# Attention with hashed buckets and a product layer: one factor operation for all pairs of heads, more operations allowed on GpSimd, and a new order

## The chip, the cores and the metric

The kernel runs on one core of one Trainium2 chip. Its time is the device time of one execution in microseconds. Beside it stands the span of a profiled execution, from its first instruction to its last. Engines are named as in the profile: PE is TensorE (PEld its weight loads), DVE is VectorE, ACT is ScalarE, POOL is GpSimd, SP is SyncE, which issues the DMAs.

## What is computed

```python
q, k, v: (4, 8, 768, 64)    proj: (64, 6)
q_bucket = sum(2**i * ((q @ proj)[..., i] > 0))         # 6 bits, the same for k
scores = where(q_bucket[:, :, :, None] == k_bucket[:, :, None, :], q @ k.T / 8, -1e9)
attn = exp(scores - max(scores));  attn /= sum(attn) + 1e-9
x = (attn @ v), heads side by side: (3072, 512)
out = ((x @ w_a) * (x @ w_b)) @ w_out                   # w_a, w_b (512, 1536), w_out (1536, 512)
```

## The kernel before, in words

Everything is done in four batches of 8 heads. A batch's queries are taken in chunks of one or two tiles of 128 rows (14 chunks in all, `CHUNKS`); each chunk has one or two halves of 8 tiles of queries (`UT`), and for each tile the scores of 768 keys are made, exponentiated, transposed and multiplied with the values. When a chunk is done, its rows go through the product layer (`moe`), with the weights resident in SBUF.

Most products are made of two float16 parts each. `power_of` finds a power of two that bounds a tensor: a Gram matrix on PE (in batch 0; squares on ACT later), its largest element on DVE (`st_k`, `st_q`, `vst`), a sum over partitions on PE (`ps_k`, `ps_q`), and two small operations on DVE (`po_t`, then `ai`: the power and its inverse). The high half is the tensor times that power in float16 (`scaled`), on ACT or DVE; the low half is what remains, on DVE (a SCALAR_TENSOR_TENSOR). `split` does that for queries and keys (tiles `qt`, `kt`), turns both halves with the rows on partitions into columns (`turn(1)`, giving `trq`, `trk`), multiplies the columns by the projection (`kb`, `qb`), takes bits of the signs (`neg_k`, `neg_q` on ACT, `bits_k`, `bits_q` on DVE), writes them as a one-hot part beside a copy of the high half (`hp`), and turns that too (`turn(0)`). In the first batch keys of all four pairs of heads and the first queries are turned by PE (transposes, copied back by ACT or DVE), later ones by DMA. The scores (`s`) then hold the penalty for unequal buckets.

`qtile` makes one tile's scores: their largest value on DVE (`mx`), a scale (`sc`) and a bias (`bias`), and the exponential on ACT (`e`). The scale holds the factor `cq`, which undoes the powers of the queries and of the keys of that pair of heads: one DVE operation for each half of a chunk and pair (line 1147), 56 in all.

The weights come in pieces of 512 KB through three staging places; each pair of pieces is rewritten by three operations (`to_f32`: a low part on ACT or POOL, a high part on ACT, and their combination on DVE, all under the name `wz`), and the next pieces wait for that. Later they are split into halves by `halved`.

No engine's order is left to chance: the program collects its operations in a list (`Plan.op`), and issues them by two tables written into the file: `ORDER`, the sequence of all operations, and `ENGINE_OF`, the engine of each that may run on several. What an operation may run on stands in its first argument (`"ACT DVE"`), and `free(b, ...)` adds POOL in batch 0 alone.

Of the kernel before, what the change touches and what calls it, by code (L numbers as in the profile page):

```python
# [20 lines left out]
P = 128  # L21
# [317 lines left out]
class Buf:  # L339
# [11 lines left out]
    @property  # L351
    def t(self):
        if self.real is None:
            if self.ring is not None:
                self.real = self.ring.pop(0)
                return self.real
            self.real = self.pool.tile(self.shape, self.dtype, tag=self.tag, name=self.name, bufs=self.bufs)
        return self.real
# [1181 lines left out]
```

## Time and profile before

| | before |
|---|---|
| median of 3 runs (lowest, highest) | 892.28 us (892.0, 892.59) |
| profiled execution, its time | 892.21 us |
| its span | 890.4 us |
| busy: PE, PEld | 869.0 us (98%), 672.4 us (76%) |
| busy: DVE, ACT, POOL | 631.1 (71%), 565.9 (64%), 438.0 us (49%) |
| chain that ended last | PE 70%, DVE 3%, issue 1% of the span |
| HBM read, written | 37.82 MB, 6.29 MB |

The busy share is that of the whole span. A stage is read by the view of stretches, which sums each engine's busy time between two moments; by the timeline, which has each instruction's start, its length, and the idle time before it with what ended it; and by the groups of instructions of one kind, which have their number and length.

### The profile page before, as it was taken

Reading aid. Unit: us, or ns where it says so; the run is one execution under the profiler, and the core shown is the slowest. Engines: PE = TensorE matmul, PEld = TensorE weight load, DVE = VectorE, ACT = ScalarE, POOL = GpSimd, SP = SyncE. Lnnn points to the kernel's source line nnn. Section 1 sums busy time; section 2 is a strip of 40 time slices with the busy share of each in tenths; the row PEclk is TensorE's granted clock in tenths of the full one; section 3 lists DMA queues with packets and bytes.
Section 4 is the critical chain, followed back from the end, with each engine's and each line's share of the span. In section 5 each row is a group of like instructions: output and inputs, shape, how many; then the busy total and the mean of one; then the engine's idle time right before and its main releaser. Section 6 shows DMA issues by size and latency. Waiting matters only on the chain.

```text
span 890.4 us, 24299 instructions
## 1 busy us (share of the span) xinstructions
PE 869.0 (98%) x9761; PEld 672.4 (76%) x9761; DVE 631.1 (71%) x1461; ACT 565.9 (64%) x1116; POOL 438.0 (49%) x371
## 2 busy tenths in 40 slices
PE   5899999999999999999999999999999999999998
PEld 4798777878777777777777777777777777777775
DVE  7998999988876766767776775767778576643311
ACT  6887767766657777667666675667676466644222
POOL 2444456447426556554454565545556457544111
PEclk9999999999999999999999999999999999999999
DMA  9989996899979979998977787799987666745100
GB/s 328 302 268 260 173 167 148 155 191 191 196 144 191 162 162 168 172 224 154 185 137 155 149 170 158 131 195 173 200 170 138 125 149 125 144 90 103 30 24 24
DMA packets 430433, 145.31 MB, mean 163 GB/s; under 512 B 404080, under 2 KB 422640, under 8 KB 430320
## 3 DMA queue, kind: packets, MB, share of 16 engines
q1 hardware_dynamic: 430160, 143.76, 79.5%
q8 instruction: 76, 1.25, 0.6%
q14 instruction: 37, 0.30, 0.1%
q10 hardware_dynamic: 160, 0.00, 0.0%
HBM read 37.82 MB, written 6.29 MB: 50 GB/s over the span
## 4 chain that ended last, share of the span: by engine, by line
PE 70%; DVE 3%; issue 1%; ACT 0%; DVEq 0%; ACTq 0%
PE ab L1371 35%; PE o L1436 17%; PE s L1136 10%; PE av L1205 8%; DVE vh L569 0%; DVE g L1400 0%; PE qb L709 0%; DVE mx L1156 0%; PE kb L709 0%; DVE hp L736 0%; DVE hp L739 0%; DVE ai_q L549 0%; DVE osb L569 0%; DVE kt L670 0%; PE ps_cx L768 0%
## 5 line engine op out<-in xcount | busy, mean ns | idle before, releaser
L1371 PE MATMUL ab<-xT,wz 128*128 128x256 f16 (+1 forms) x3456 | 377.2, 264 | 1.0 <-DVE g L1400 0.8
L563 POOL TENSOR_TENSOR a<-e,a 128x768 f16<-128x768 f32 x170 | 286.2, 1687 | 186.7 <-ACT a L560 84.0
L1371 PEld LDWEIGHTS <-wz 128*128 128x128 f16 x3456 | 310.4, 98 | 49.5 <-issue 1.5
L1177 ACT ACTIVATE e<-s,bias,sc 128x768 f32<-128x768 f32 x192 | 189.7, 988 | 110.3 <-DVE bias L1168 93.0
L1156 DVE TENSOR_REDUCE mx<-s 128x1 f32<-128x768 f32 x192 | 182.6, 953 | 53.2 <-PE s L1136 49.1
L1436 PE MATMUL o<-wz,g 128*128 128x512 f16 (+1 forms) x840 | 215.8, 392 | 0.2 <-DVE g L1400 0.2
L1416 POOL TENSOR_TENSOR g<-g,g 128x256 f16<-128x256 f32 x132 | 94.8, 718 | 191.1 <-ACT g L1411 185.5
L1136 PE MATMUL s<-trk,trq 76*128 76x384 f16 (+1 forms) x768 | 155.0, 327 | 2.4 <-ACT e L1177 1.8
L1400 DVE SCALAR_TENSOR_TENSOR g<-ab,ab,a 128x256 f32<-128x256 f32 x132 | 63.4, 480 | 105.1 <-ACT a L1392 87.2
L1205 PEld LDWEIGHTS <-at 128*128 128x128 f16 x3312 | 117.5, 98 | 16.5 <-issue 2.7
L1436 PEld LDWEIGHTS <-g 128*128 128x128 f16 x792 | 73.9, 98 | 68.7
L1392 ACT ACTIVATE a<-ab,ab 128x256 f32<-128x256 f32 x132 | 62.1, 470 | 99.5 <-PE ab L1371 86.6
L1205 PE MATMUL av<-vh,at 128*128 128x64 f16 x2208 | 121.9, 193 | 0.0
L1136 PEld LDWEIGHTS <-trq 76*128 76x128 f16 (+1 forms) x768 | 70.6, 98 | 44.1 <-issue 6.8
L1411 ACT CAST g<-g 128x256 f16<-128x256 f32 x132 | 53.0, 402 | 59.0 <-DVE g L1400 48.5
L560 ACT CAST a<-e 128x768 f16<-128x768 f32 x102 | 84.5, 829 | 3.0 <-DMA at<-a 1.2
L1205 PE MATMUL av<-vl,at 128*128 128x64 f16 x1104 | 62.4, 193 | 0.0
L1363 PE MATMUL ab<-xT,wz 128*128 128x128 f32 x384 | 49.4, 279 | 0.0
L560 DVE CAST a<-e 128x768 f16<-128x768 f32 x68 | 39.4, 580 | 14.0 <-ACT e L1177 14.0
L1363 PEld LDWEIGHTS ab<-xT,wz 128*128 128x128 f32 x384 | 46.2, 192 | 3.4 <-issue 2.2
L1168 DVE TENSOR_SCALAR bias<-mx,sc 128x1 f32<-128x1 f32 x181 | 38.8, 214 | 6.4
L1164 DVE TENSOR_SCALAR sc<-mx,cq 128x1 f32<-128x1 f32 x181 | 38.3, 211 | 4.8
(171 smaller groups left out, 793.7 us busy)
## 6 DMA issues: line engine op xcount, KB each, us to landing
rq<-in_q_dram SPq DMA_DIRECT2D x24, 256.0 KB, 3.5
rk<-in_k_dram SPq DMA_DIRECT2D x16, 384.0 KB, 3.9
wz<-in_moe_w_a_dram SPq DMA_DIRECT2D x12, 512.0 KB, 5.9
wz<-in_moe_w_b_dram SPq DMA_DIRECT2D x12, 512.0 KB, 5.0
wz<-in_moe_w_out_dram SPq DMA_DIRECT2D x12, 512.0 KB, 5.6
out_dram<-osb SPq DMA_DIRECT2D x24, 256.0 KB, 2.4
vr<-in_v_dram SPq DMA_DIRECT2D x12, 384.0 KB, 4.4
at<-a SPq DMA_TRANSPOSE x184, 3.6
```

The costliest lines, as they stand in the source:

```text
L560: {"ACT": nc.scalar.copy, "DVE": nc.vector.tensor_copy, "POOL": nc.gpsimd.tensor_copy}[e](out=out, in_=x)
L563: (nc.gpsimd if e == "POOL" else nc.vector).tensor_tensor(out=out, in0=x, in1=y, op=ALU.subtract)
L1136: nc.tensor.matmul(ps.t[:, jj, :HALF], lhsT=trq.t[rows, i, (2 * j + h) * nt + t], rhs=tr.t[rows, i, k0 : k0 + NT // 2].rearrange("p n s -> ...
L1156: lambda: nc.vector.tensor_reduce(out=mx.t[:, col], in_=halves(ps.t), axis=AX.XY, op=ALU.max, negate=True),
L1177: lambda: nc.scalar.activation(flat2(e.t), halves(ps.t), AF.Exp, bias=bias.t[:, col], scale=sc.t[:, col], accum_out=sm.t[:, u : u + 1],),
L1205: nc.tensor.matmul(av.t[:, u, :], lhsT=at.t[:, a + kt, :], rhs=w.t[:, h, kt, :], start=i == 0, stop=i == 3 * NT - 1,)
L1363: nc.tensor.matmul(pl.t[:, m, to], lhsT=wt32(m, cc, f), rhs=xt.t[:, cc * nt // NC, cc * nt % NC : cc * nt % NC + nt, :], start=cc == 0, st ...
L1371: nc.tensor.matmul(pl.t[:, m, to], lhsT=wt(m, wi, cc, f), rhs=xt.t[:, cc * nt // NC, xi, cc * nt % NC : cc * nt % NC + nt, :], start=i == ...
L1392: lambda a=a, pl=pl, gr=gr, sc_of=sc_of: nc.scalar.activation(a.t, pl.t[:, 0, :CH], AF.Copy, scale=sc_of(gr)),
L1400: lambda a=a, g32=g32, pl=pl, gr=gr, sc_of=sc_of: nc.vector.scalar_tensor_tensor(out=g32.t, in0=pl.t[:, 1, :CH], scalar=sc_of(gr + 1), in1 ...
L1416: lambda g=g, g32=g32, g_of=g_of: nc.gpsimd.tensor_tensor(out=g_of(g[1]), in0=g32.t, in1=g_of(g[0]), op=ALU.subtract),
L1436: nc.tensor.matmul(po[u].t.rearrange("p a b -> p (a b)"), lhsT=x()[:, us], rhs=w, start=f == 0 and i == 0, stop=f == NF - 1 and i == len(t ...
```

## The change

The factors `cq` of all pairs of a half are made by one operation: the keys' powers of a batch get one tile (`k_ai`, one row of two numbers for each pair), and the operation reads the inverses of its pairs from it. In the first chunk alone there is still one operation for each pair. That makes 27 operations where there were 56. The pool `po_ai` shrinks from 14 buffers to 10. High halves (of queries, keys and values in batch 0, and of weights) and the cast of a chunk's output in batch 0 may also run on POOL. The constants of the power are listed as waiting for the projection. And both tables are new.

```diff
 ORDER = (
-    2, 1, 75, 11, 76, 4, 3, 77, 5, 78, 79, 80, 81, 0, 12, 13, 14, 15, 6, 282, 281, 9, 10, 84, 27, 16, 82, 17, 83, 18,
+    1, 2, 4, 3, 75, 76, 5, 77, 9, 78, 11, 79, 80, 6, 7, 12, 13, 14, 279, 0, 15, 16, 17, 278, 280, 281, 81, 10, 84, 18,
...
+class Part(tuple):
+    @property
+    def t(self):
+        return self[0].t[:, self[1]]
...
-    op("DVE", 0.4, pw_consts, -79, w=["pw"])
+    op("DVE", 0.4, pw_consts, -79, r=[("pj", 0), ("pj", 1)], w=["pw"])
...
-        ai = keep or buf("po_ai", [P, 2], F32, f"ai_{name}", 14)
+        ai = keep or buf("po_ai", [P, 2], F32, f"ai_{name}", 10)
...
             nc.scalar.activation(out, x, AF.Copy, scale=by)
         else:
-            nc.vector.tensor_scalar(out=out, in0=x, scalar1=by, scalar2=None, op0=ALU.mult)
+            (nc.gpsimd if e == "POOL" else nc.vector).tensor_scalar(
+                out=out, in0=x, scalar1=by, scalar2=None, op0=ALU.mult
+            )
...
-            "ACT DVE", {"ACT": 0.3 + 0.83e-3 * size, "DVE": 0.24 + 0.54e-3 * size},
+            *free(b, ACT=0.3 + 0.83e-3 * size, DVE=0.24 + 0.54e-3 * size, POOL=0.2 + 1.01e-3 * size),
             high, key, r=[*toks, ai] + ["csb"] * len(first), w=[(pt[0], "hi"), *first], sbuf=True,
...
-            "ACT DVE", {"ACT": 1.24, "DVE": 0.75}, lambda e: scaled(e, hi(), z(), al_of(ai)),
+            "ACT DVE POOL", {"ACT": 1.24, "DVE": 0.75, "POOL": 1.24}, lambda e: scaled(e, hi(), z(), al_of(ai)),
...
-                "ACT DVE", {"ACT": 0.95, "DVE": 0.65}, lambda e: scaled(e, flat(vh), x(), al_of(ai)),
+                *free(b, ACT=0.95, DVE=0.65, POOL=0.95), lambda e: scaled(e, flat(vh), x(), al_of(ai)),
...
+        if hp == 0:
+            kinv[b] = buf("k_ai", [P, NPAIR, 2], F32, f"k_ai{b}")
...
-        if h == 0 and t == 0:
+
+        js = slice(j, j + 1) if m == 0 else slice(0, UT // 2 // nt)
+        if h == 0 and t == 0 and js.start == j:
+            hps = slice(hp, hp + js.stop - js.start)
             op(
                 "DVE", 0.16,
                 lambda: nc.vector.tensor_scalar(
-                    out=cq.t[:, j : j + 1], in0=inv_of(qinv[m, half]), scalar1=inv_of(kinv[b, hp]), scalar2=0.125,
+                    out=cq.t[:, js], in0=kinv[b].t[:, hps, 1], scalar1=inv_of(qinv[m, half]), scalar2=0.125,
                     op0=ALU.mult, op1=ALU.mult,
...
-                "ACT DVE", {"ACT": 0.65, "DVE": 0.44}, lambda e: cast(e, t2.t[:, :w], flat()), key, r=[x],
+                *free(b, ACT=0.65, DVE=0.44, POOL=0.65), lambda e: cast(e, t2.t[:, :w], flat()), key, r=[x],
```

What the tables do is seen in the order of the instructions. The first place is ACT, from its fifth instruction on: `hp`, `trq` and `trk` are the copies of the first queries' and keys' halves and of their turned columns, `wz` the weights. Before:

```order
L560 COPY hp_76<-qt_0_0_111 128x8x64
L560 COPY trq_0_153<-qt_0_0_143 128x1024
L560 COPY trk_0_168<-kt_0_0_155 128x1536
L876 ACTIVATE wz<-wz 128x1024 x2
L560 COPY hp_77<-kt_0_0_140 128x12x64
L727 COPY neg_k_0_229<-kb_0_199 128x72
L727 COPY neg_q_0_231<-qb_0_217 128x48
L866 ACTIVATE wz<-wz 128x1024
```

and with the change:

```order
L875 ACTIVATE wz<-wz 128x1024
L885 ACTIVATE wz<-wz 128x1024
L567 COPY hp_77<-kt_0_0_138 128x12x64
L567 COPY trk_0_187<-kt_0_0_148 128x1536
L567 COPY trq_0_205<-qt_0_0_161 128x1024
L736 COPY neg_k_0_210<-kb_0_189 128x72
L885 ACTIVATE wz<-wz 128x1024
L736 COPY neg_q_0_229<-qb_0_214 128x48
L885 ACTIVATE wz<-wz 128x1024
```

The weights' low and high part (lines 875 and 885) come ahead of the first copies, and a third part (line 885) stands between `neg_k` and `neg_q`.

The second place is DVE, from the second keys' largest element (`st_k_1`) on, with the halves of `kt_0_1` and the one-hot parts of the first pair. Before:

```order
L583 TENSOR_REDUCE st_k_1_189<-gram_k_1_171 128x1
L546 TENSOR_SCALAR po_t_k_1_194<-ps_k_1_191 128x1
L549 SCALAR_TENSOR_TENSOR ai_k_1_195<-pw,po_t_k_1_194 128x2
L569 TENSOR_SCALAR kt_0_1_212<-rk_1_138,ai_k_1_195 128x12x64
L670 SCALAR_TENSOR_TENSOR kt_0_1_212<-rk_1_138,ai_k_1_195,kt_0_1_212 128x12x64
L884 SCALAR_TENSOR_TENSOR wz<-wz 128x1024
L583 TENSOR_REDUCE st_k_3_242<-gram_k_3_235 128x1
L730 TENSOR_TENSOR bits_k_0_261<-kb_0_199,neg_k_0_229 128x72
L736 TENSOR_SCALAR hp_77<-bits_k_0_261 128x12x6
L739 TENSOR_SCALAR hp_77<-bits_k_0_261 128x12x6
```

and with the change:

```order
L592 TENSOR_REDUCE st_k_1_207<-gram_k_1_180 128x1
L893 SCALAR_TENSOR_TENSOR wz<-wz 128x1024
L553 TENSOR_SCALAR po_t_k_1_226<-ps_k_1_223 128x1
L556 SCALAR_TENSOR_TENSOR k_ai_135<-pw,po_t_k_1_226 128x2
L739 TENSOR_TENSOR bits_q_0_231<-qb_0_214,neg_q_0_229 128x48
L576 TENSOR_SCALAR kt_0_1_233<-rk_1_170,k_ai_135 128x12x64
L679 SCALAR_TENSOR_TENSOR kt_0_1_233<-rk_1_170,k_ai_135,kt_0_1_233 128x12x64
L592 TENSOR_REDUCE st_k_3_246<-gram_k_3_238 128x1
L739 TENSOR_TENSOR bits_k_0_248<-kb_0_189,neg_k_0_210 128x72
```

A weights' combination (line 893) and the query bits (`bits_q`, which need `neg_q`) come ahead of the second keys' halves.

The third place is PE, around the products that give the bits of the first pair (`kb`, `qb`). Before, from the second keys' Gram matrix on:

```order
L596 MATMUL gram_k_1_171<-rk_1_138 128x128
...
L534 MATMUL ps_k_1_191<-st_k_1_189,onesr 128x1
...
L534 MATMUL ps_k_1_191<-onev,onesr 128x1
...
L709 MATMUL kb_0_199<-pjw_67,trk_0_168 128x12
...
L709 MATMUL qb_0_217<-pjw_68,trq_0_153 128x12
...
L596 MATMUL gram_k_3_235<-rk_3_233 128x128
```

and with the change (weight loads and repeated rows are left out in both):

```order
L605 MATMUL gram_k_1_180<-rk_1_170 128x128
...
L718 MATMUL kb_0_189<-pjw_67,trk_0_187 128x12
...
L718 MATMUL qb_0_214<-pjw_68,trq_0_205 128x12
...
L541 MATMUL ps_k_1_223<-st_k_1_207,onesr 128x1
...
L541 MATMUL ps_k_1_223<-onev,onesr 128x1
...
L605 MATMUL gram_k_3_238<-rk_3_236 128x128
```

The sum of the second keys' bound (`ps_k_1`) has moved behind `qb`.

## Rows read from the trace of the kernel before

**Rows 1.** The page's first part: busy time, share of the span and instructions by engine.
```profile
PE 869.0 (98%) x9761; PEld 672.4 (76%) x9761; DVE 631.1 (71%) x1461; ACT 565.9 (64%) x1116; POOL 438.0 (49%) x371
```

**Rows 2.** View by stretches: from:to, length, busy us (instructions) of PE, PEld, DVE, ACT, POOL, clock.
```profile
0.00:10.00 10.00, 2.98 (x27) 2.42 (x28) 4.87 (x19) 2.62 (x6) 2.70 (x7) 1.00 0.82 283
10.00:20.00 10.00, 8.42 (x101) 7.78 (x100) 9.26 (x27) 9.46 (x12) 2.44 (x2) 1.00 1.04 358
20.00:28.00 8.00, 6.60 (x48) 5.03 (x46) 7.48 (x18) 6.11 (x8) 3.16 (x3) 1.00 1.02 356
28.00:40.00 12.00, 9.78 (x132) 7.92 (x131) 11.79 (x29) 9.96 (x15) 5.84 (x7) 1.00 0.98 290
40.00:62.00 22.00, 21.70 (x211) 19.51 (x211) 21.61 (x46) 18.84 (x34) 7.41 (x9) 1.00 0.83 271
62.00:294.00 232.00, 228.34 (x2805) 181.42 (x2803) 199.73 (x444) 161.54 (x304) 120.67 (x102) 1.00 0.93 183
294.00:880.00 586.00, 584.68 (x6411) 444.47 (x6409) 374.60 (x881) 354.93 (x738) 294.44 (x243) 1.00 0.75 143
```

**Rows 3.** Timeline of PE: start us, length us, line, operation, count, [idle before, releaser].
```profile
13.00 0.36 PE L709 MATMUL qb<-pjw,trq 128*128 128x12 f16 x8
...
14.56 1.46 PE L688 MATMUL kt<-identh,kt 128*128 128x128 f16 x12 [0.50 <-DVE kt L670]
...
21.93 1.44 PE L688 MATMUL kt<-identh,hp 128*128 128x128 f16 x12 [0.38 <-ACT trq L560]
23.17 1.48 PE L1136 MATMUL s<-trk,trq 76*128 76x384 f16 x4
...
26.16 0.84 PE L596 MATMUL gram_v<-v 128*128 128x128 bf16 x6
...
28.24 0.83 PE L688 MATMUL kt<-identh,kt 128*128 128x128 f16 x12
```

**Rows 4.** Factors and powers (min/median/max ns); POOL groups (busy us, mean ns).
```profile
L1147 DVE TENSOR_SCALAR cq<-ai_q,ai_k x56: 198/205/216, 19.8 to 727.4; 128x1 f32<-128x1 f32 x56
...
L549 DVE SCALAR_TENSOR_TENSOR ai_q<-pw,po_t_q x24: 220/233/1685, 5.5 to 725.8; 128x2 int32<-128x2 f32 x24
...
L563 POOL TENSOR_TENSOR a<-e,a 128x768 f16<-128x768 f32 x170 | 286.2, 1687 | 186.7 <-ACT a L560 84.0 <-DVE a L560 59.4 <-issue 13.1
...
L560 POOL CAST a<-e 128x768 f16<-128x768 f32 x14 | 13.3, 952 | 4.5 <-ACT e L1177 2.7 <-issue 1.6
```

**Rows 5.** Timeline of ACT, the first 16 us.
```profile
9.78 1.01 ACT L560 COPY trq<-qt 128x1024 f16<-128x1024 f16 x1 [2.93 <-PE qt L688]
11.16 1.44 ACT L560 COPY trk<-kt 128x1536 f16<-128x1536 f16 x1 [0.37 <-PE kt L688]
12.50 2.18 ACT L876 ACTIVATE wz<-wz 128x1024 f32<-128x1024 f32 x2
14.58 0.81 ACT L560 COPY hp<-kt 128x768 f16<-128x768 f16 x1
...
15.41 0.18 ACT L727 COPY neg_q<-qb 128x48 f32<-128x48 f32 x1
15.50 1.12 ACT L866 ACTIVATE wz<-wz 128x1024 int32<-128x1024 uint8 x1
```

**Rows 6.** Timeline of POOL: the first weights' low part.
```profile
8.68 1.90 POOL L868 TENSOR_SCALAR wz<-wz 128x1024 int32<-128x1024 uint8 x1 [6.78 <-DMA wz<-in_moe_w_a_dram]
```

**Rows 7.** Timeline of DVE, the first 16 us.
```profile
9.71 0.87 DVE L549 SCALAR_TENSOR_TENSOR ai_pj<-pw,po_t_pj 128x2 int32<-128x2 f32 x1
...
12.38 0.16 DVE L546 TENSOR_SCALAR po_t_k<-ps_k 128x1 f32<-128x1 int32 x1 [0.28 <-PE ps_k L534]
...
12.83 0.62 DVE L569 TENSOR_SCALAR kt<-rk,ai_k 128x768 f16<-128x768 f32 x1
13.49 1.02 DVE L670 SCALAR_TENSOR_TENSOR kt<-rk,ai_k,kt 128x768 f16<-128x768 f32 x1
14.42 1.22 DVE L884 SCALAR_TENSOR_TENSOR wz<-wz 128x1024 int32<-128x1024 int32 x1
```

More of the change, by code (lines that the diff above doesn't have):

```diff
@@ L628, in attention_moe, with split @@
         )
-    def split(raw, x, n, side, b, key, toks, tag, by_pe=()):
+    def split(raw, x, n, side, b, key, toks, tag, by_pe=(), keep=None):
         which = "kq"[side]
@@ L655, in split @@
             gram(lambda: raw.t[:, :size], size, key, toks, lambda: stat.t, stat, tag, f"{which}{x}")
-        ai = power_of([lambda: stat.t], [stat], f"{which}{x}", key, tag, True)
+        ai = power_of([lambda: stat.t], [stat], f"{which}{x}", key, tag, True, keep)
         def high(e):
@@ L1050, in kprep @@
         raw = load_pair(k, b, hp, f"rk_{b}_{hp}", key - 1)
-        trk[b, hp], kinv[b, hp] = split(raw, f"{b}_{hp}", NK, 0, b, key, [raw], tag, () if b else K_PE.get(hp, ()))
+        if hp == 0:
+            kinv[b] = buf("k_ai", [P, NPAIR, 2], F32, f"k_ai{b}")
+        trk[b, hp], _ = split(
+            raw, f"{b}_{hp}", NK, 0, b, key, [raw], tag, () if b else K_PE.get(hp, ()), Part((kinv[b], hp))
+        )
     def heads(m, half):
@@ L1147, in qtile @@
                 lambda: nc.vector.tensor_scalar(
-                    out=cq.t[:, j : j + 1], in0=inv_of(qinv[m, half]), scalar1=inv_of(kinv[b, hp]), scalar2=0.125,
+                    out=cq.t[:, js], in0=kinv[b].t[:, hps, 1], scalar1=inv_of(qinv[m, half]), scalar2=0.125,
                     op0=ALU.mult, op1=ALU.mult,
                 ),
-                key - 1, r=[qinv[m, half], kinv[b, hp]], w=[(cq, j)],
+                key - 1, r=[qinv[m, half]] + [(kinv[b], x) for x in range(NPAIR)[hps]],
+                w=[(cq, x) for x in range(UT // 2)[js]],
             )
```

453 rows, old and new, of tables (ENGINE_OF, ORDER) are left out of this document.

## The prediction

> **What bounds the kernel now.** The first view is the busy time of the engines: TensorE (PE) is busy 869.0 us of a span of 890.4 us, 98% [rows 1]. Neither the matmuls' number nor their shapes change (9761 before and after), so the time can move only by what PE does not do in the other 21.4 us, and by how fast its clock runs. The view by stretches says where these lie [rows 2]: 7.0 us idle in the first 10 us, 1.6 up to 20, 1.4 up to 28 (10.0 in all by 28), 2.2 from 28 to 40, 0.3 from 40 to 62, 3.7 from 62 to 294, 1.3 in the 586 us from 294 to 880, and about 4 at the end, where the last outputs leave. The start is therefore the stage to read. There the timeline of PE [rows 3] shows two things. Twelve transposes of 128x128 take 1.46 us at 14.56 and 1.44 at 21.93, and 0.83 us at 28.24: up to 28 us PE ran at half speed (1.2 GHz), from then on at 2.4, though the column of the granted clock in [rows 2] stands at 1.00 throughout. And the first matmul of scores starts at 23.17 us, behind a chain that passes through all engines. VectorE (DVE) is busy 11.79 of 12 us from 28 to 40 and 21.61 of 22 up to 62 [rows 2]: in the start it is as full as PE.
>
> The profiled execution took 892.21 us, 1.8 more than its span, and lies 0.07 us under the median of the three runs shown (892.28); the sum is made against 892.21. What a measurement of this kernel can tell from no change is about 0.2%, 1.8 us.
>
> **The change, part by part.** *From 294 us on* the rows of PE, ScalarE (ACT), GpSimd (POOL) and SyncE stand in the same order before and after, and DVE only lacks operations of 0.2 us while it is busy 375 of 586 us [rows 2]. This stretch costs and gives nothing, and so does the end: a lead or a delay at 294 us is the result.
>
> *One operation for the factor of queries and keys.* 56 operations of 0.205 us on DVE [rows 4] become 27. That takes 29 x 0.2 = 5.9 us from DVE over the span; of these 11 are of batch 0 (20 become 9) and some 4 more lie before 294 us, 15 x 0.2 = 3.1 us. They lie beside PE's work; they count only where DVE is the one that is waited for.
>
> *GpSimd for high halves and casts.* The new list gives it ten such operations: three high halves of queries, one of keys, two of values, two of weights, two casts of outputs. The list moves other operations too: 7 pairs of one-column operations (scale and bias) leave DVE for GpSimd, and 5 remainders, larger ones, go from GpSimd to DVE; I set these two against each other and a little more, and count DVE as about 2 us lighter up to 294 us, between 0 and 5.9. The trace has no high half on GpSimd. The nearest rows are its cast of 128x768, 0.95 us, and its subtraction of the same size, 1.69 us [rows 4]; I take 0.95, since the new operation reads one tensor, as the cast does, and keep 1.69 as the upper end. For the halves of queries, two thirds that size, either is a bound from above.
>
> *The new order at the start.* This I follow by hand with durations of rows. ACT now takes the first weights' low and high part (1.12 and 2.18/2 = 1.09) before it has copied anything of queries and keys, and they land at 8.68, when GpSimd starts on them now [rows 5, 6]. So: 8.68 + 1.12 + 1.09 = 10.9; copy of the keys' high half 0.81, 11.7; copy of the first keys (trk) 1.44, 13.1, where it ended at 12.6; of the queries (trq) 1.01, 14.15, where it ended at 10.8. PE takes its instructions in order: the query bits (qb, 0.36) now start at 14.2 instead of 13.00, and the bound of the second keys (ps_k), which had been ahead of them, stands behind them and ends at 14.7. On DVE its power of two follows, at 14.8 where it ran at 12.38 (0.16 and 0.22, 15.2 with the steps between), and then, new, the query bits, which wait for ACT: neg_k, as long as neg_q, 0.18, another weights' high part 1.09, neg_q 0.18, so 15.6. Behind this wait DVE holds the second keys' two halves: 15.6 + 0.2 + 0.62 + 1.02 = 17.5, where the low half ended at 14.5 [rows 7]. PE's second transposes of keys start at 17.5 instead of 14.56 [rows 3]: 2.9 us late.
>
> From there: transposes 1.46, ACT's copy 1.44, key bits 0.36 x 12/8 = 0.54, neg_k 0.18: 21.1. DVE meanwhile does a weights' combination of 1.22 and eight small operations of about 0.2 each (the size of the factor's and of the power's, [rows 4]): 20.4 with the steps between; GpSimd's high half of the fourth keys 0.95, 21.3; DVE's low half 1.02, then a second combination of 1.22 and seven small ones: 25.0. PE transposes 1.44, a Gram matrix of four products (0.84 for six [rows 3], so 0.56), and the first scores start at 27.1 instead of 23.17, 3.9 us late. In between PE has done one Gram matrix of values (0.84) more. So PE has 3.9 - 0.84 = 3.1 us more idle time by 28 us, all of it at half speed. What is left undone is then done at full speed, so it costs 3.1 x 0.83/1.44 = 1.8 us. From 28 to 40 us I find the waits about equal (by the same steps: 0.6 for a copy of the third keys, 1.0 for exponentials, 0.3 for one-hot parts, against 2.2 now). **Start: +1.8 us.** Bounds: +0.6, if the two weights' parts on ACT land early enough to cost nothing beyond the 2 us of the second half of this chain; +3.1, without the discount for the clock.
>
> *GpSimd beside DVE.* The same DVE operation, the two numbers of a power of two, takes 0.22 us as a rule and 0.87 at 9.71 us, while GpSimd's operation of 8.68 to 10.58 runs [rows 6, 7]; the longest took 1.69 [rows 4], as long as a GpSimd subtraction. So each GpSimd operation in the start can hold a DVE operation with two inputs for 0.65 us; I count one such in the path at half its size: **+0.3 us**, between 0 and 1.3 (two at full size). The Trainium skill, SBUF — State Buffer, section Who interferes with whom, states that a VectorE instruction with two SBUF inputs and a GpSimd instruction that reads SBUF exclude each other for the whole instruction; by it the block in the path counts at its full 0.65, and the sum would be +2.5 rather than +2.1. No run here yet shows a high half beside it.
>
> *From 40 to 294 us* PE idles 4.0 us now. DVE is 2 us lighter, but is waited for in small pieces; I take 0, and bounds of -2.0 (half of the idle time gone) and +2.0 (a placement as much worse).
>
> The sum is 1.8 + 0.3 + 0 = +2.1: 892.2 + 2.1 = **894.3 us**; its own range is 893.2 to 895.6.
>
> **The rivals.** *Paid back.* The lighter DVE gives back in 40 to 294 us what the start loses, up to 2 of the 4.0 us: 892.2 us, 891 to 893.2. For it: DVE at 98% from 28 to 62 us [rows 2]. Against: PE idles only 0.3 us from 40 to 62, so there is little to be had just there.
>
> *Faster.* The chain above is too slow by some 2 us because an operation stands less in the way than I count, the start is then even, and DVE's lightness closes two thirds of the 4.0 us: 892.2 - 2.6 = 889.6. It decides if the first scores start before about 24 us. For it: the new order does its Gram matrices of values in gaps at half speed. Against: the waits on neg_q and on GpSimd's half are plain in the order.
>
> *The clock rises later.* PE had worked without a gap from 21.93 us when the clock rose at 28 [rows 3]. In the new order I find a gap up to 25.0, 3 us later. If the rise comes 3 us later too, PE's work in these costs (1 - 0.83/1.44) x 3 = 1.3 more: 895.6. The Trainium skill, TensorE: Matmul & The Clock Gate, Part 1, says that half speed is the resting state and that sustained work releases it, with a moment that varies from run to run. By that page this rival is open until a run shows it; the three runs, 0.6 us apart, speak against much chance in it.
>
> *More on GpSimd than it can hide.* With halves of 1.69 instead of 0.95 us, four of them before 62 us that DVE waits for, 4 x 0.74 = 3.0 more: 897.3.
>
> *The change does not do what it says.* It does, as far as an order can tell: 27 factors, and ten operations on GpSimd that it could not have before.
>
> **How the numbers follow.** Forecast 0.36 (of it 0.08 under 894.0, within 0.2%); paid back 0.24; faster 0.22; later clock 0.10; GpSimd 0.08. Slower by over 0.2%: 0.28 + 0.18 = 0.46; within: 0.08 + 0.24 = 0.32; faster: 0.22. The range runs from 889.2, which takes in the faster case's own time and leaves out what lies below it, to 897.5.
>
> **What would show it.** Right: the first scores start near 27 us, DVE waits for neg_q at 15 us, PE's idle time by 28 us is near 13 us, and from 294 us on every row lies later by the same 2 us. Wrong: the first scores before 24 us, transposes at 0.83 us well before or after 28, or PE idle time from 40 to 294 us far from 4.0.

## The result: 0.84% slower, in four pieces

The changed kernel takes 899.49 us (median of 4 runs, 899.34 to 900.1), the one before 892.14 us (4 runs, 891.62 to 892.59): the ratio is 1.0084, its 95% interval 1.0066 to 1.0101. The direction was forecast, the size (+2.1 us) was not, and 899.49 lies outside the range of 889.2 to 897.5. The profiled execution of the changed kernel took 899.34 us, its span is 897.5 us, 7.1 more than before.

The first part of its page, and the view by stretches with the same bounds as in [rows 2]:

```profile
PE 869.7 (97%) x9761; PEld 671.9 (75%) x9761; DVE 629.7 (70%) x1416; ACT 568.2 (63%) x1121; POOL 449.2 (50%) x382
```

```profile
0.00:10.00 10.00, 2.13 (x19) 1.66 (x20) 4.11 (x18) 2.77 (x5) 2.96 (x7) 1.00 0.82 276
10.00:20.00 10.00, 7.13 (x81) 6.50 (x79) 7.47 (x27) 8.11 (x11) 1.95 (x2) 1.00 1.04 400
20.00:28.00 8.00, 5.70 (x56) 4.54 (x54) 5.08 (x13) 5.58 (x7) 3.24 (x2) 1.00 1.04 324
28.00:40.00 12.00, 9.71 (x139) 8.51 (x138) 10.38 (x24) 11.36 (x16) 1.70 (x3) 1.00 0.54 176
40.00:62.00 22.00, 21.60 (x215) 19.43 (x213) 19.04 (x41) 19.89 (x36) 11.18 (x13) 1.00 0.98 296
62.00:294.00 232.00, 226.58 (x2762) 180.06 (x2762) 199.50 (x414) 157.76 (x296) 128.77 (x110) 0.99 0.94 179
294.00:880.00 586.00, 583.22 (x6411) 442.16 (x6410) 381.45 (x880) 359.04 (x748) 296.69 (x244) 1.00 0.81 145
```

PE's work is the same (869.7 against 869.0 us), so the time is again in what PE does not do and in its clock. Idle time by 28 us: 7.87 + 2.87 + 2.30 = 13.0 us, where it was 10.0. From 28 to 62 us 2.7 against 2.5. From 62 to 294 us 5.4 against 3.7, and the clock column shows 0.99 there. After 294 us, 2.8 against 1.3.

**The start** came nearly as forecast. The timeline of PE, and below it rows of ACT, POOL and DVE, of the changed kernel:

```profile
17.22 1.46 PE L697 MATMUL kt<-identh,kt 128*128 128x128 f16 x12 [1.57 <-DVE kt L679]
...
25.01 1.44 PE L697 MATMUL kt<-identh,hp 128*128 128x128 f16 x12 [1.72 <-DVE hp L748]
...
26.67 1.48 PE L1149 MATMUL s<-trk,trq 76*128 76x384 f16 x4
...
28.64 1.18 PE L697 MATMUL kt<-identh,kt 128*128 128x128 f16 x12
...
9.01 1.14 ACT L875 ACTIVATE wz<-wz 128x1024 int32<-128x1024 uint8 x1 [3.01 <-DMA wz<-in_moe_w_a_dram]
...
19.46 2.22 POOL L576 TENSOR_SCALAR kt<-rk,k_ai 128x768 f16<-128x768 f32 x1 [4.36 <-DVE k_ai L556]
...
15.38 0.21 DVE L739 TENSOR_TENSOR bits_q<-qb,neg_q 128x48 f32<-128x48 f32 x1 [0.28 <-ACT neg_q L736]
...
21.71 1.02 DVE L679 SCALAR_TENSOR_TENSOR kt<-rk,k_ai,kt 128x768 f16<-128x768 f32 x1 [2.00 <-POOL kt L576]
```

The second transposes of keys stand at 17.22 us (forecast 17.5, before 14.56 [rows 3]), DVE waits for `neg_q` until 15.38 (forecast 15.6) and for GpSimd's high half until 21.71 (forecast 21.3), and the first scores start at 26.67 (forecast 27.1, before 23.17). The twelve transposes at 28.64 take 1.18 us: the clock rose within them. The trace's record of the granted clock begins at 29.36 us; before, it begins at 28.0.

**The middle** has something new. The rows of POOL, SyncE's queue, ACT and PE around 150 us, and the stretches with their clock column:

```profile
144.08 2.86 POOL L576 TENSOR_SCALAR wz<-wz,w_ai 128x1024 f16<-128x1024 f32 x1
146.92 2.36 POOL L570 TENSOR_TENSOR a<-e,a 128x768 f16<-128x768 f32 x1
...
149.31 1.41 SPq L1111 DMA_TRANSPOSE at<-a  x1
150.82 0.84 SPq L947 DMA_DIRECT2D rk<-in_k_dram  x1
151.77 1.45 SPq L1111 DMA_TRANSPOSE at<-a  x1
...
153.06 0.83 ACT L567 CAST a<-e 128x768 f16<-128x768 f32 x1 [2.75 <-DMA at<-a]
153.80 0.98 ACT L1194 ACTIVATE e<-s,bias,sc 128x768 f32<-128x768 f32 x1
...
154.93 0.81 PE L1149 MATMUL s<-trk,trq 76*128 76x384 f16 x4 [1.86 <-ACT e L1194]
155.58 3.54 PE L1380 MATMUL ab<-xT,wz 128*128 128x128 f32 x16
```

```profile
153.00:155.60 2.60, 0.74 (x6) 0.47 (x5) 1.67 (x4) 2.54 (x4) 2.07 (x2) 1.00 1.08 271
155.70:159.00 3.30, 3.30 (x18) 3.24 (x17) 2.94 (x5) 2.67 (x5) 0.54 (x1) 0.50 1.56 201
```

In the first of these stretches PE had no wait before:

```profile
153.00:155.60 2.60, 2.60 (x37) 2.50 (x36) 2.46 (x8) 1.71 (x4) 1.23 (x1) 1.00 0.63 141
```

Read upwards from PE: scores wait 1.86 us for an exponential on ACT; ACT had waited 2.75 us with a cast ahead of it, for a buffer that a transposing DMA frees; that DMA is the one issued at 149.31, as soon as GpSimd's remainder of 146.92 (what the float16 part of an exponential leaves) was done, and the cast starts when it has landed, at 153.06; the remainder, itself 2.36 us instead of the usual 1.69 [rows 4], had waited behind a high half of weights, 2.86 us long. Right behind the wait PE's clock stands at 0.50: full until 155.66, half until 159.07 by the trace's record. PE lost 1.86 us by waiting and 3.4 / 2 = 1.7 by the clock.

**The end** was to change nothing. But the scores that lay 6.15 us late at 318 us lie 7.12 us late at 821 us. Two waits that PE had before as 0.36 us, shown below the two, and not at all:

```profile
505.91 0.81 PE L1149 MATMUL s<-trk,trq 76*128 76x384 f16 x4 [0.74 <-ACT e L1194]
...
735.78 1.46 PE L1453 MATMUL o<-wz,g 128*128 128x512 f16 x6 [0.35 <-DVE g L1417]
```

```profile
499.22 0.81 PE L1136 MATMUL s<-trk,trq 76*128 76x384 f16 x4 [0.36 <-ACT e L1177]
```

To add the pieces up I count PE's work by 62 us as its busy time at full speed plus half of that at half speed: 40.5 us before, 38.1 now. So the start cost 2.4, the waits from 62 to 294 us 1.8 more than before, the half-speed stretch 1.7, the end 1.0: 6.9 of the 7.1 us. By idle time the end is 1.5 (2.8 against 1.3), since PE also waits 0.79 us at 299.8, ahead of the scores at 318; then the sum is 7.4.

### The profile page after: what moved, and what is told of

Its sections match the earlier page's. It is cut to its first block, busy times and chain, and to the rows that moved or that the text cites. A ratio compares the mean times of both kernels' runs of the same rounds, so it can differ in the third digit from the quotient of the medians.

```text
span 897.5 us, 24262 instructions
## 1 busy us (share of the span) xinstructions
PE 869.7 (97%) x9761; PEld 671.9 (75%) x9761; DVE 629.7 (70%) x1416; ACT 568.2 (63%) x1121; POOL 449.2 (50%) x382
## 4 chain that ended last, share of the span: by engine, by line
PE 82%; DVE 9%; issue 3%; DMA 2%; ACT 2%; POOL 1%; SPq 0%; ACTq 0%; DVEq 0%
PE ab L1388 36%; PE o L1453 19%; PE s L1149 12%; PE av L1222 9%; PE ab L1380 3%; DVE mx L1173 2%; DMA at<-a 1%; ACT wz L885 1%; DVE g L1417 1%; DMA wz<-in_moe_w_a_dram 1%; DVE wz L893 1%; DMA wz<-in_moe_w_out_dram 1%; PE av L1207 1%; DVE wz L836 1%; PE kt L697 0%
## 5 line engine op out<-in xcount | busy, mean ns | idle before, releaser
L570 POOL TENSOR_TENSOR a<-e,a 128x768 f16<-128x768 f32 x167 | 280.0, 1681 | 178.8 <-ACT a L567 73.7
L1409 ACT ACTIVATE a<-ab,ab 128x256 f32<-128x256 f32 x132 | 62.1, 471 | 97.6 <-PE ab L1388 83.4
L567 DVE CAST a<-e 128x768 f16<-128x768 f32 x69 | 42.2, 611 | 15.8 <-ACT e L1194 15.6
```

Source lines behind the costliest of these rows:

```text
L567: {"ACT": nc.scalar.copy, "DVE": nc.vector.tensor_copy, "POOL": nc.gpsimd.tensor_copy}[e](out=out, in_=x)
L570: (nc.gpsimd if e == "POOL" else nc.vector).tensor_tensor(out=out, in0=x, in1=y, op=ALU.subtract)
L1409: lambda a=a, pl=pl, gr=gr, sc_of=sc_of: nc.scalar.activation(a.t, pl.t[:, 0, :CH], AF.Copy, scale=sc_of(gr)),
```

## The experiments

All kernels but e1, e3 and e8 are the changed kernel with the edit shown. Theory G is that GpSimd's high halves, slower than the order was made for, are the loss; theory O that the order itself is. Single executions of one kernel differ by some 4 us (the one before from 890.87 to 894.44 us, e14 from 896.88 to 901.32), so differences of a microsecond between medians of four decide nothing, and the traces are read beside them.

**e1: the merge alone.** The new code with the order and the engines of before, renumbered for the 29 operations that are gone; its first line:

```diff
 ORDER = (
-    1, 2, 4, 3, 75, 76, 5, 77, 9, 78, 11, 79, 80, 6, 7, 12, 13, 14, 279, 0, 15, 16, 17, 278, 280, 281, 81, 10, 84, 18,
+    2, 1, 75, 11, 76, 4, 3, 77, 5, 78, 79, 80, 81, 0, 12, 13, 14, 15, 6, 279, 278, 9, 10, 84, 27, 16, 82, 17, 83, 18,
...
```

> Only the factors are merged (56 operations to 27); order and engines of all other operations are those of before. Both theories: 891.0 to 892.5 us, no difference that can be measured, because the 29 operations of 0.2 us that go lie beside PE's work. If it came out above 894, the merged operation itself would hold something up, and both theories would be wrong.

892.77 us, ratio 1.0009 (0.9998 to 1.0021): no difference that can be measured, 0.3 us above the range expected. The smaller pool and the constants' new dependency are in this kernel too, so they cost nothing that shows. But its trace has a cost that no theory had. The group of merged factors on DVE, then one of them with GpSimd's operations beside it:

```profile
L1166 DVE TENSOR_SCALAR cq<-k_ai,ai_q 128x2 f32<-128x2 f32 x20 | 9.6, 481 | 0.5
```

```profile
726.40 1.57 DVE L1166 TENSOR_SCALAR cq<-k_ai,ai_q 128x2 f32<-128x2 f32 x1
...
724.70 3.25 POOL L573 TENSOR_TENSOR a<-e,a 128x768 f16<-128x768 f32 x2
```

The factor of one column took 0.20 to 0.22 us, all 56 of them [rows 4]. That of two columns takes 0.48 on average: 5 of 20 last 0.60 to 1.57 us, and the one shown, issued right behind the start of GpSimd's second remainder, ends with it (727.95 and 727.97). From 312 to 814 us this kernel falls from 1.06 to 0.24 us ahead of the one before, with the same two waits (0.74 and 0.36) as the changed kernel. Instead of 5.9 us the merge takes 11.6 - 11.1 = 0.5 us from DVE. The Trainium skill, VectorE: DVE Perf Modes, section Mode 2×_2P, says that an operation with one source, all of it in SBUF, can run on both of DVE's SBUF ports where the outermost dimension longer than one is even, and SBUF — State Buffer, section Who interferes with whom, that one of these ports is GpSimd's as well and is held for a whole instruction. The rows agree as far as they go: in each of the 13 profiles with the merged factor 4 to 6 of the 20 operations of two columns take over 0.4 us, each ending with a GpSimd operation, and no factor of one column took over 0.22 us in any of the 17 profiles. The operations of four columns, which the rule covers too, three in each of the 13 profiles, were never seen held (0.27 us at most).

**e7: the factors singly.**

```diff
-                lambda: nc.vector.tensor_scalar(
-                    out=cq.t[:, js], in0=kinv[b].t[:, hps, 1], scalar1=inv_of(qinv[m, half]), scalar2=0.125,
-                    op0=ALU.mult, op1=ALU.mult,
-                ),
+                lambda: [
+                    nc.vector.tensor_scalar(
+                        out=cq.t[:, c : c + 1], in0=inv_of(qinv[m, half]), scalar1=kinv[b].t[:, p, 1:2], scalar2=0.125,
+                        op0=ALU.mult, op1=ALU.mult,
+                    )
+                    for c, p in zip(range(js.start, js.stop), range(hps.start, hps.stop))
+                ],
```

> The changed kernel, but each merged factor is issued as its two or four operations of one column, in the same place. Theory H: the operation of two columns is held by GpSimd (5 of 27 took 0.60 to 1.65 us, each until the end of the GpSimd operation beside it), that of one column is not (56 of 56 took 0.20 to 0.22 us before): all factors take about 0.2 us, PE's wait at 505 us shrinks from 0.74 to 0.36 us and that of 0.35 us at 735 us goes: 898.5 to 899.0 us. Against it: the operation is held because of what it reads or where it stands, the long ones stay and the time is 899.5 to 900 us.

897.50 us (896.54 to 899.1), below the ranges of both theories. In the trace theory H holds: all 56 operations are short again, the wait at 506 us is 0.48, that at 735 us is gone, and from 318 to 821 us it loses 0.2 us to the kernel before where the changed kernel lost 1.0. So the merged form costs 0.8 us there. The 13 profiles with it have a wait of 0.74 us for those scores, the four without it 0.36 to 0.48. What else of the 2.0 us between the medians there is, the trace does not show (its profiled execution took 899.1 us); it can be the spread between executions.

```profile
L1166 DVE TENSOR_SCALAR cq<-ai_q,k_ai 128x1 f32<-128x1 f32 x56 | 9.0, 205 | 0.4
```

**e2 and e3: the ten operations on GpSimd, taken out and put in.** e2 is the changed order with the ten back on ACT and DVE; e3 the order of before with the ten on GpSimd. The change moves 112 other operations between engines too; no run takes these back without the order.

```diff
 ENGINE_OF = {
...
     "POOL": (
-        64, 80, 105, 111, 521, 527, 622, 694, 844, 1008,
...
```

> The changed kernel with its own order, but the ten operations that GpSimd got (eight high halves, two casts) are back on the engines (ACT or DVE) that had them before. Theory G (GpSimd's high halves take 1.6 to 2.9 us, two to three times what the order was made for, and make the waits in 62 to 294 us): 893 to 895.5 us, the 1.9 us gap of PE at 153 us and the half-speed stretch behind it are gone. Theory O (the order itself is worse, at the start and after it, whoever does the ten): 898 to 900 us, the gap stays.

> The order of before with the merged factor, but the ten operations (eight high halves, two casts) on GpSimd. Theory G: 895 to 900 us, since the slow operations stand in an order that was not even made for them. Theory O: 891 to 893 us.

e2: 901.66 us (900.85 to 902.67), worse than with them, and outside both expectations. The wait at 153 us is down to 0.80 and 0.39 us and the half-speed stretch is gone, as G said, but other waits stand in their place:

```profile
27.64 1.48 PE L1153 MATMUL s<-trk,trq 76*128 76x384 f16 x4
...
58.88 0.81 PE L1153 MATMUL s<-trk,trq 76*128 76x384 f16 x4 [1.15 <-ACT e L1198]
...
98.87 0.20 PE L545 MATMUL ps_w<-wst,onesr 128*128 128x1 bf16 x2 [1.23 <-DVE wst L596]
```

e3: 902.25 us (900.35 to 904.57), worse still, and again outside both: PE waits 2.04 us at 58 us, and its clock is at 0.50 from 62.1 to 68.9. Each of the two orders loses with the other's engines for the ten. Theory G is too coarse: as a set, the ten are worth 2 us to the new order, slow as they are.

**e11: how slow, and why.** The groups of GpSimd's high halves in the changed kernel, and in e11, where they are products of two tensors:

```diff
-    gpsimd.tensor_scalar(out=out, in0=x, scalar1=by, scalar2=None, op0=ALU.mult)
+    gpsimd.tensor_tensor(out=out, in0=x, in1=by.to_broadcast(list(x.shape)), op=ALU.mult)
```

> The changed kernel, but GpSimd makes the high halves by a product of two tensors (the second is the power, one column read again and again) instead of by a product with one number for each partition. What GpSimd's own rows say: a difference of two tensors of 128x768 takes 1.69 us, the high half of 128x768 2.22 us. Theory F (the form with one number for each partition is what is slow): 1.1 us for 128x512, 1.7 for 128x768, 2.2 for 128x1024; 897 to 899 us. Theory X (float32 in and float16 out with a factor is slow in any form): the same 1.6, 2.2 and 2.9 us; 899 to 900.5 us.

```profile
L576 POOL TENSOR_SCALAR vh<-v,v_ai 128x768 f16<-128x768 f32 x2 | 5.1, 2564 | 0.2
L576 POOL TENSOR_SCALAR qt<-rq,ai_q 128x512 f16<-128x512 f32 x3 | 4.8, 1597 | 5.1 <-DVE ai_q L556 4.4 <-DVE cq L1163 0.6
L576 POOL TENSOR_SCALAR wz<-wz,w_ai 128x1024 f16<-128x1024 f32 x1 | 2.9, 2863 | 0.0
```

```profile
L579 POOL TENSOR_TENSOR vh<-v,v_ai 128x768 f16<-128x768 f32 x2 | 3.6, 1802 | 0.2
L579 POOL TENSOR_TENSOR qt<-rq,ai_q 128x512 f16<-128x512 f32 x3 | 3.1, 1042 | 5.2 <-DVE ai_q L558 4.5 <-DVE cq L1166 0.6
L579 POOL TENSOR_TENSOR wz<-wz,w_ai 128x1024 f16<-128x1024 f32 x1 | 1.9, 1890 | 0.0
```

Theory F holds for the durations: the form with one number for each partition takes 1.60, 2.56 and 2.86 us, the product of two tensors 1.04, 1.80 and 1.89, a third less. The time hardly follows: 899.06 us (898.02 to 900.61), at the upper end of what it forecast. The chain through the DMA and ACT is shorter, as it should be (ACT's cast waits 0.64 us instead of 2.75), but PE waits 1.89 us at 152 us all the same, now for DVE, and the clock still falls behind it:

```profile
149.88 1.71 DVE L1352 TENSOR_SCALAR ab<-fw,x_mx 128x6 f32<-128x6 f32 x1
...
153.94 1.57 PE L1383 MATMUL ab<-xT,wz 128*128 128x128 f32 x8 [1.89 <-DVE g L1420]
```

This DVE operation takes 0.53 us in the changed kernel. Here it stands beside GpSimd's operations, which come earlier, and it ends with one of them (151.59 and 151.56): the shorter half only hands the wait on to another engine.

**e5: the one half in the chain.** Only the weights' half of 144 us goes to ACT.

```diff
 ENGINE_OF = {
     "ACT": (
...
+        521,
...
     "POOL": (
...
-        521,
```

> The changed kernel, but one operation, the high half of a piece of weights that runs on GpSimd at 144.08 us for 2.86 us, is on ACT (the engine that had it before). Theory W: that operation delays GpSimd's remainders of a, these the transposing DMAs (queued in order on SP), these the cast on ACT that waits 2.75 us, and that the scores that PE waits 1.86 us for at 153 us; after that wait the granted clock stands at half for 3.4 us. So the gap and the half-speed stretch go: 899.5 - 1.9 - 1.7 = 895.9 us (895 to 897). Theory S (a wait of this size comes in another place whatever is done to one operation, as in the kernel with all ten moved back): 898.5 to 900 us.

897.13 us (896.53 to 897.56), ratio to the one before 1.0053 (1.0036 to 1.007). Theory W, 0.1 us above its range: the wait of 1.86 us is now two of 0.47 and 0.39, and the clock stays at 1.00.

```profile
153.06 1.16 PE L1382 MATMUL ab<-xT,wz 128*128 128x128 f32 x8 [0.47 <-DVE g L1419]
...
154.61 0.81 PE L1151 MATMUL s<-trk,trq 76*128 76x384 f16 x4 [0.39 <-ACT e L1196]
```

```profile
155.70:159.00 3.30, 3.30 (x43) 3.02 (x42) 3.23 (x6) 3.27 (x7) 0.00 (x0) 1.00 1.40 149
```

It gave 2.4 us, not 3.6: 1.86 - 0.86 + 1.7 = 2.7 is what these rows say. So one operation of 2.86 us, on an engine that is half idle, cost some 2 us by where it stood; with e11, where a shorter one in the same place cost nearly as much, its length alone was not the cause.

**e4 and e8: the start, exchanged.** e4 has the order and engines of before for its first 216 operations (its `ORDER` begins as that of e1), and then the changed order; e8, the mirror of it, begins as the changed kernel for 218 operations and goes on as e1.

> The changed kernel, but its first 216 operations (up to the scores of the first chunk, some 45 us) in the order and on the engines of before. By the sum of the two traces the start cost 2.3 us (3.0 us idle at half speed, worth 1.8, and the clock that rose 1.4 us later, worth 0.6): 897.2 us, with the gap at 153 us and the half-speed stretch still there, by both theories. If the later stretch hung on the start's delay, it would be under 895.

> The merged factor, the first 218 operations in the order and on the engines of the changed kernel, all later ones in the order and on the engines of before. The mirror of the run with the start of before, which came out 4.3 us under the changed kernel: if the start has a price of its own, 892.8 + 2.8 to 4.3 = 895.6 to 897.1 us. If the rest of before's order takes a late start back (PE waits for less where it comes later), 892.5 to 894.5 us.

e4: 895.19 us (894.53 to 896.54), 4.3 less where 2.3 was expected. Its first scores start at 22.42 us, and its clock stands at full speed for 3.4 us at 19 us and again from 25.98. The wait of 1.86 us and the half-speed stretch behind it are there as before (at 152 us). e8: 897.39 us (896.96 to 899.12), 5.0 above the one before; 1.7 of it is again a half-speed stretch, from 52.1 to 55.5, behind a wait of 1.43 us where the two orders meet. e4 shows that the start has a price of its own, larger than its idle time (13.55 us by 62 us in its profile, against 15.73). e8 agrees, but bounds it less well: its half-speed stretch and 1.7 us of idle time from 28 to 62 us (4.4 against 2.7) come from the seam.

**e6, e10, e13, e14: the steps of the start, singly and together.** e6 has the fourth keys' high half on DVE, e10 undoes the three steps of order that the prediction named, e13 moves the second turn behind the scores, e14 does all of it. First e10 (280 to 282 are the parts of the weights, 30 the bound, 86 and 87 the query bits), then e13 (41 is the turn, 42 its copy, 123 the scores), then e6:

```diff
-    1, 2, 4, 3, 75, 76, 5, 77, 9, 78, 11, 79, 80, 6, 7, 12, 13, 14, 279, 0, 15, 16, 17, 278, 280, 281, 81, 10, 84, 18,
-    82, 27, 8, 20, 28, 19, 21, 284, 94, 83, 29, 282, 22, 283, 286, 85, 30, 31, 86, 87, 32, 33, 59, 60, 293, 61, 23,
+    1, 2, 4, 3, 75, 76, 5, 77, 9, 78, 11, 79, 80, 6, 7, 12, 13, 14, 279, 0, 15, 16, 17, 278, 81, 10, 84, 18, 82, 27,
+    8, 20, 28, 19, 21, 284, 94, 83, 280, 281, 29, 30, 31, 32, 33, 283, 85, 22, 86, 286, 282, 87, 59, 60, 293, 61, 23,
...
-    90, 133, 296, 95, 96, 40, 25, 36, 26, 48, 52, 49, 41, 152, 194, 42, 195, 123, 196, 299, 197, 124, 125, 91, 92,
+    90, 133, 296, 95, 96, 40, 25, 36, 26, 48, 52, 49, 152, 194, 195, 123, 41, 42, 196, 299, 197, 124, 125, 91, 92,
...
     "POOL": (
-        52, 64, 80, 105, 111, 125, 135, 144, 154, 182,
+        52, 80, 105, 111, 125, 135, 144, 154, 182,
```

> The changed kernel, but the high half of the fourth keys, 2.22 us on GpSimd from 19.46 us, for which DVE idles 2.0 us, is on DVE (0.62 us). Theory G (GpSimd's slow halves on the start's chain): the first scores start near 25.3 us instead of 26.67, and the time is 898.1 to 898.9 us. Theory O (the other waits of the new order hold the chain just as long): first scores at 26.4 us or later, 899.0 to 900.0 us.

> The changed kernel with the three steps of the start undone that the prediction named, all else as it was: ACT's low and high part of the first weights behind the copies of keys and queries (and their combination on DVE behind the second keys' halves), the second keys' bound ahead of the query bits on PE, the query bits on DVE behind the second keys' halves. Theory C (these steps are what makes the start late): second transposes of keys near 15 us instead of 17.2, first scores 2 to 3.5 us earlier than 26.67 (23.2 to 24.7), time 1 to 2.5 us less: 897 to 898.5 us. Theory D (something later in the start holds the first scores, as the fourth keys' high half on GpSimd): transposes near 15 us, but first scores at 25.7 us or later and less than 1 us gained.

> The changed kernel, but the second turn of the second keys on PE (25.01 us, for which PE waits 1.72 us on DVE's one-hot part) and its copy on ACT stand behind the first scores. Theory P (the first scores are ready by 24.8 us, when ACT has copied the first keys, and wait only because this turn stands ahead of them in PE's order): first scores near 25 us instead of 26.67, 0.5 to 1.5 us gained, 897.9 to 898.9 us. Theory Q (the wait only moves behind the scores): first scores near 25 us, time 899 to 900 us.

> Five edits of the start together: the three named steps (weights' parts behind the copies on ACT, bound ahead of the query bits on PE, query bits behind the second keys' halves on DVE), the fourth keys' high half on DVE, and the second turn behind the scores. Theory P: first scores at 23 to 24.5 us, PE's idle time by 28 us near 11 us (13.0 in the changed kernel), 896.5 to 898 us. Theory Q: first scores earlier, but idle time up to 40 us still 14 to 15 us, 898.5 us or more; then what the start of before has is not these steps but its order as a whole.

e6: 898.09 us (895.62 to 900.6), first scores at 25.99, between its two theories, and too wide to decide. e10: 901.09 us (898.55 to 901.56), theory D: the second transposes start 0.9 us earlier (not 2, as both theories had it), but the first scores at 27.05. The first row is of DVE, the others of PE:

```profile
13.71 0.87 DVE L558 SCALAR_TENSOR_TENSOR k_ai<-pw,po_t_k 128x2 int32<-128x2 f32 x1
...
16.34 0.84 PE L699 MATMUL kt<-identh,kt 128*128 128x128 f16 x12 [1.44 <-DVE kt L681]
...
25.39 1.44 PE L699 MATMUL kt<-identh,hp 128*128 128x128 f16 x12 [2.38 <-DVE hp L750]
...
27.05 1.48 PE L1151 MATMUL s<-trk,trq 76*128 76x384 f16 x4
```

The power of the second keys takes 0.87 us instead of 0.22 and ends with GpSimd's operation beside it (14.58): the block that the prediction priced at 0.65 us, here in the path. What holds the scores there is a turn of the *second* keys, ahead of them in PE's order, which waits 2.38 us for DVE, which had waited for GpSimd. (Not all of its time is the start's: at 190 us PE waits 1.78 us for a DMA, 1.76 in e6, as in no other profile.) e13 moves it: first scores at 24.37, but 899.77 us (897.98 to 901.73), theory Q. e14: first scores at 24.93, PE's idle time by 28 us 12.5 us, and 900.0 us (896.88 to 901.32), theory Q. The scores come 1.7 us earlier and the time does not: half speed lasts until 36.0 us in its profile, but for 3.4 us.

**e9, e15, e12: the base again, and the sums.** e9 is the changed kernel unaltered; e15 is e14 with e5 and e7; e12 is e4 with e5 and e7.

> The changed kernel once more, as the base of the runs beside it, since single executions of one kernel differ by up to 2 us where the clock of PE goes up and down in the first 40 us. All theories: 899 to 900.5 us, the half-speed stretch behind a wait of 1.86 us near 153 us again.

> The same five edits of the start, and with them the weights' high half of 144 us on ACT and the factors singly. By the terms of the runs before (-2.4 and -0.8 to -2.0 beside the start): 3 to 4 us under the run with the start alone, 893 to 895 us under theory P, 895 to 896.5 us under theory Q.

> Three edits together: the first 216 operations as before, the weights' high half of 144 us on ACT, the factors singly. Alone they gave -4.3, -2.4 and -2.0 us (the last with 0.8 us less of late waits in the trace). If the three are separate terms: 899.5 - 4.3 - 2.4 - 0.8 to 2.0 = 890.8 to 892.0 us, with no half-speed stretch after 40 us. If they are one and the same loss seen from three sides: 894 to 895 us.

e9: 899.18 us (897.41 to 900.19), with the same wait (1.87 us at 152.7) and the half-speed stretch behind it.

e12: 892.19 us (10 runs, 890.99 to 893.45), against 892.27 for the kernel before beside it, ratio 0.9993 (0.9984 to 1.0003). That is 0.2 us above the range for separate terms, and far from the 894 of one loss seen three times: on the start of before, the three edits together take back the whole loss. How it splits is less sure. Alone they gave 4.3 (start), 2.4 (the half at 144 us) and 0.8 to 2.0 (factors); the first pair of traces says 2.4, 3.5 and 1.0. Its stretches show the early full speed of before's start (0.65 in the clock column) and idle times of 3.9 and 1.4 us in the last two, as before:

```profile
20.00:28.00 8.00, 5.61 (x47) 4.26 (x46) 7.46 (x18) 6.09 (x8) 3.17 (x3) 0.65 1.01 350
...
62.00:294.00 232.00, 228.12 (x2802) 181.13 (x2801) 202.31 (x435) 162.70 (x307) 124.13 (x109) 1.00 0.95 182
294.00:880.00 586.00, 584.59 (x6407) 444.07 (x6406) 374.08 (x881) 355.48 (x739) 295.07 (x243) 1.00 0.80 143
```

No version beat both kernels.

e15: 899.05 us (897.57 to 899.58), far above the 893 to 896.5 expected, and 0.95 under e14 instead of 3 to 4. Its later waits are as short as they should be (1.4 us idle from 294 to 880 us, 3.0 in e14), and e14 had no half-speed stretch at 157 us to lose; what is missing beyond that is at the start. The timeline of PE says why:

```profile
25.03 1.48 PE L1151 MATMUL s<-trk,trq 76*128 76x384 f16 x4
...
33.38 1.49 PE L699 MATMUL kt<-identh,kt 128*128 128x128 f16 x12
...
39.31 0.83 PE L699 MATMUL kt<-identh,hp 128*128 128x128 f16 x12 [0.54 <-DVE hp L750]
```

Twelve transposes still take 1.49 us at 33.38; the clock's record begins at 37.36. This start has 0.9 us less idle time by 62 us than e9 and 9 us more at half speed.

A table of the profiled executions puts the starts side by side (us; half speed by the trace's clock record, before its first entry taken as half). It leaves out e2 and e3, which have the ten on other engines, and e8, whose seam lies before 62 us:

| start | kernels | first scores | idle by 62 | half speed by 62 | PE's work by 62 |
|---|---|---|---|---|---|
| of before | before, e1, e4, e12 | 22.4 to 23.2 | 12.5 to 13.7 | 28.0, 22.6, 22.6, 22.1 | 40.5, 42.0, 41.3, 42.0 |
| of the change | after, e5, e7, e9, e11 | 26.0 to 26.7 | 15.0 to 16.2 | 29.4, 27.4, 26.2, 28.4, 28.2 | 38.1, 38.2, 38.7, 38.9, 39.0 |
| of the change, edited | e6, e10, e13, e14, e15 | 26.0, 27.1, 24.4, 24.9, 25.0 | 15.5, 16.7, 16.2, 15.2, 14.3 | 29.8, 30.8, 27.4, 32.6, 37.4 | 36.9, 36.0, 37.8, 36.5, 35.7 |

On average the change's start does 41.42 - 38.56 = 2.9 us less work by 62 us. It has 2.3 us more idle time, worth 1.2 at half speed, and 4.1 us more at half speed, worth 2.05 where PE works through it: together a little over the 2.9. The last line shows that idle time alone does not set the price. Which of the start's steps does is not shown: undoing five of them (e14) gave nothing back, only before's order and engines as a whole did (e4, e12).

## Why the prediction was right and wrong

1. **Order at the start, idle time: right.** 3.1 us more by 28 us were forecast, 3.0 measured; the first scores within 0.4 us. Two of its sizes were off and cancelled: GpSimd's high half took 2.22 us instead of 0.95, and DVE reached it at 19.5 instead of 20.4.
2. **The clock at the start: priced as a rival, and it came.** "The clock rises later" had a chance of 0.10 at 1.3 us. It rose 1.35 us later in the first profile (0.6 us), and over nine profiles the new start had about 4 us more at half speed. It is not an alternative to the forecast, it came on top of it; that more waits bring less full speed is not shown (e15 has the least idle time of the changed starts and the most half speed). With it the start is 2.4 us by the first pair of profiles, 2.9 by nine profiles, against 2.1 forecast with the term for GpSimd beside DVE, which the start's chain showed as 0.05 us (a power of two in 0.27 us instead of 0.22, at 14.83); in e10 it came at its full 0.65.
3. **From 40 to 294 us: "I take 0", the step that failed.** It cost 3.5 us: 1.8 of waits and 1.7 of a half-speed stretch. Its bound of 2.0 took a placement as costing idle time alone. Behind it is the price of a high half on GpSimd: "I take 0.95 ... and keep 1.69 as the upper end" was taken from a cast, and it measured 1.59 to 1.61 for 512 columns, 2.2 to 2.9 for 768, 2.85 to 2.86 for 1024. Even the upper end was too low: neither of the nearest rows multiplies by one number for each partition, and as a product of two tensors the same half took 1.47 us (e11). The rival "more on GpSimd than it can hide" (0.08, 897.3) had the right engine, with too small a price, in the wrong place: it looked before 62 us, and it bit at 144 us, through a transposing DMA and a cast on ACT. e5 shows that taking this one operation away removes most of the wait and the half speed; e11 shows that a shorter one does not, so the step that failed is the placement taken as free, more than the price of the half.
4. **From 294 us on "costs and gives nothing": wrong by 1.0 to 1.5 us.** The same order of rows was taken for the same times. Of the operations that differ, the 27 merged factors, 5 take 0.60 to 1.65 us, held beside GpSimd's; with single factors (e7) 0.8 of the 1.0 goes.
5. **Factors: 5.9 us lighter on DVE, measured 0.6** (11.56 to 10.94 us), for the same reason. The rivals "paid back" and "faster" rested on that lightness; DVE is busy 199.5 us from 62 to 294 us where it was 199.7.

The sum forecast +2.1; by the same steps it should have been 2.4 + 3.5 + 1.0 = 6.9. The direction came out right, but 4.5 of the 6.9 came from stretches for which it had forecast nothing.

## What to carry to other kernels

Price an operation on an engine by a row of the same form: on GpSimd the product with one number for each partition took 2.22 us where a cast of the same shape took 0.95, and a product of two tensors a third less. A merge that widens a small operation from one column to two can cost more than it saves when GpSimd works beside it. On a kernel that PE bounds, a new wait of 1.4 to 2 us should be priced twice, once as idle time and once as the half speed that may follow (it did in eight of sixteen here). And in an order made for one set of engines, moving operations is a gamble until it is measured: ten put in cost 9.5 us (e3 against e1), ten taken out 2 (e2), one taken out gained 2.4 (e5).

## What the runs showed of the hardware that was not expected

- **Clock after a wait.** Nine profiles have a wait of 1.86 to 1.89 us at about 150 to 156 us. In six (after, e4, e7, e9, e11, e13) the clock stood at half for 3.4 us behind it, in three (e6, e10, e14) it did not. In e3 it fell for 6.8 us behind a wait of 2.04, in e8 for 3.4 behind 1.43; before, a wait of 1.49 us at 234 us had no such follow-up, nor had four of 1.69 to 1.78 us at 107 to 243 us in e3, e6 and e10. That makes eight of sixteen. What decides is not settled.
- **Clock at the start.** In ten of the seventeen profiles PE had full speed for some microseconds early (the first such stretch lies between 11.9 and 24.6 us), then half again. It stood at full for good, or up to a later wait, from 25.5 us on at the earliest and from 41.0 at the latest. In e15 PE worked from 25 to 37 us with no wait over 0.9 us and stayed at half. Why it rises so late there stays open; some of the spread between executions of one kernel may come from there, but no run separates it.
- **DVE held for two columns of one source**, beside a GpSimd operation and until its end: 0.58 to 1.65 us instead of 0.2, in 13 of 13 profiles that have such factors, and for one column in none of 17.
